# Attention feeding a mixture of experts on one core: three count operations from VectorE to GpSimd, and one router sum split over two steps

## The chip, the core and the metric

The kernel runs on one core of a Trainium2 chip. A core has five engines that run side by side and wait for each other through semaphores: PE (TensorE, matrix products into PSUM), DVE (VectorE), ACT (ScalarE), POOL (GpSimd) and SP (SyncE, which here only issues DMAs). Each engine executes its instructions in the order in which the program gives them to it. POOL also issues DMAs: those whose rows are addressed by an index (scatters and gathers), and those that add to what lies in SBUF.

The metric is the device time of one execution in microseconds; the times given are medians of several runs. The profiler records one execution more, whose span runs from its first to its last instruction.

## The reference

Eight batches of eight heads, 576 tokens each, 64 wide, go through causal attention with a decay bias. The result, 4608 rows of 512, is routed row by row to one of eight experts.

```python
def _attn_ref(q, k, v, s):
    scores = scale * np.matmul(q, k.transpose(0, 1, 3, 2))
    s_pos = np.maximum(s, 0.0)
    cum = np.cumsum(s_pos, axis=-1)
    bias = -(cum[:, :, :, None] - cum[:, :, None, :])
    scores = np.where(causal, -1000000000.0, scores + np.minimum(bias, 0.0))
    scores = scores - np.max(scores, axis=-1, keepdims=True)
    attn = np.exp(scores)
    attn = attn / (np.sum(attn, axis=-1, keepdims=True) + 1e-09)
    return np.matmul(attn, v)
...
def _moe_ref(x, expert_emb, tau, w1, w2):
    xn = x / (np.linalg.norm(x, axis=-1, keepdims=True) + 1e-06)
    en = expert_emb / (np.linalg.norm(expert_emb, axis=-1, keepdims=True) + 1e-06)
    logits = xn @ en.T / tau
    expert_idx = np.argmax(logits, axis=1)
...
    for e in range(E):
        mask = expert_idx == e
        h = np.maximum(x[mask] @ w1[e], 0.0)
        out[mask] = gate_w[mask, None] * (h @ w2[e])
```

## The kernel before

**Tiling.** A batch is called a block, `b` = 0 to 7, and a head `n` = 0 to 63, so block 7 is heads 56 to 63. The 576 query rows of a head are five tiles of 128 (the last one half full); the index `j` counts them. Four heads make a group, whose queries and keys are loaded together.

**Steps.** `step(n)` emits the work of one head for all engines, and steps follow one another. In step `n`, PE makes the transposed scores of head `n` in two PSUM tiles, `ta` and `tb` (`ta_`, `tb_`, `tbm`, `tbl`), and the scores of head `n`+5 in the other orientation, from which DVE takes the row maxima (`s1` to `s4`, `sa`, `sb`; the reductions are on lines 360, 397 and 400). ACT takes the exponentials of head `n` into one of three buffers `P32` (lines 488 and 491). POOL writes the low part of them, PL (`pl_`, line 242 by way of `psub`): 576 columns at the end of step `n`, 1024 at the beginning of step `n`+1. From step 58 on, part of the second piece is done by DVE instead (line 498). In step `n`, PE also makes the value product of head `n`-2 (`pv`, lines 516 to 518) into the PSUM bank `om`; it reads both the exponentials and PL. In step `n`+3, DVE divides the product of head `n` by its row sums (`norm1` to `norm3`, lines 529, 533, 541), writes the rows of the block (`xt`) and so frees `om` for the next product.

**DMAs of POOL.** The scores are made from high and low parts of queries and keys. The low parts come from a DMA that adds the fp32 input from DRAM to the negated rounded copy in SBUF (`addl`, line 329): for the group that comes next, into KC in the group's first step and into QC in its second one. So step 53 (second head of its group) issues the one into QC for heads 56 to 59, and step 57 the one into QC for heads 60 to 63. `ta_` and `tb_` of those heads read QC and KC on line 454.

**Router.** When the last head of block `b` has been normalised, in step 8`b`+10, `router(b, xt)` appends small tasks to a list. `slots(4)`, near the end of each step, takes up to four of them and stops at a `None`. In order: `sume` (sum of the products with the expert vectors for all five tiles, eight sums for each row; line 74, by way of `esum`), `sel1` (maximum, line 598), `None`, `sel2`, `sel3` (lines 602, 605), `None`, `sel4`, `sel5` (lines 609, 613), and `rank` into the list `mq`. `mslot`, in the middle of the next step, runs `rank`: ten small matmuls (`rank0`), and `rank1` to `rank3` go to the front of the task list, where `slots(4)` of the same step takes them. They give each row its place in its expert's table `xs` (`pos`, line 641). After that five scatters (line 659), one for each `j`, are free to be issued, one to five of them a step.

For block 5 (`b == nb - 3`) `rank1` also copies the count of expert 0 (line 633), and `rank3` works out from it the indices of the first three gathers, `cnt0`, `gi0` and `va0` (lines 643 to 645). Block 5's sum stands in step 50, its ranks in step 53. Block 6's sum stands in step 58, its ranks in step 61.

**First gathers.** In step 61, `tail` issues three gathers of expert 0's first 384 rows (`xload`, line 722), which use `gi0`; `va0` is read in `xstat`, some 30 us later. From step 56 on SP loads expert weights (line 798).

**What sets the order.** The order on each engine is the order of the program text, written out by hand (`manual_schedule`); the framework adds the waits. Near the end of step 53 the program has:

```python
        if n < NH:
            slots(4)
...
        later()
        if live and c == 0:
            addl(g + 1, True)
        if live and c == 1:
            addl(g + 1, False)
        mrow1(m)
        if live:
            pl_(n, 0, 576, "p")
```

Of the kernel before, what the change touches and what calls it, by code (L numbers as in the profile page):

```python
# [15 lines left out]
ALU = mybir.AluOpType  # L16
# [24 lines left out]
XW = 576  # L41
# [3 lines left out]
NBIG = 1 << 20  # L45
# [26 lines left out]
def esum(nc, L, x):  # L72
    e = x.rearrange("p j (q a e) -> p j e q a", q=4, e=NE)[:, :, :, :, ::17]
    nc.vector.tensor_reduce(L, e, AX.XY, ALU.add)
# [32 lines left out]
def main(ctx, tc, qkh, qkc, vtin, s_in, emb, tau, w1h, w2h, out, shared, nb):  # L107
    nc = tc.nc
# [102 lines left out]
    IX = {}  # L211
# [323 lines left out]
    def norm3(n):  # L535
        if n not in HD:
            return
        b, hh = n // H, n % H
        xt, z, ov = XT[b], HD[n]["z"], HD[n]["ov"]
        o = 72 * hh  # L540
        nc.vector.tensor_tensor(xt[:, :, o:o + 72], ov[:, :, 1 - hh % 2:73 - hh % 2], z.unsqueeze(2).to_broadcast([128, 5, 72]), op=ALU.mult)  # L541
        del HD[n]
        if hh == H - 1:
            nc.gpsimd.tensor_copy(xt[:, :, XW:XR].bitcast(I32), IX["recf"][:, b].unsqueeze(2).to_broadcast([128, 5, XR - XW]))
            nc.gpsimd.tensor_copy(xt[:, :, XW + 1:XW + 3], VB[b]["ws"].unsqueeze(1).to_broadcast([128, 5, 2]))
            router(b, xt)
# [42 lines left out]
    def router(b, xt):  # L589
        R = {}  # L590

        def sume():
            R["L"] = om[:, 416:456].rearrange("p (j e) -> p j e", j=5)
            esum(nc, R["L"], xt[:, :, 0:XW])

        def sel1():
            m = R["m"] = p2.tile([128, 2, 5], F32, name="rm", bufs=1)
            nc.vector.tensor_reduce(m[:, 0], R["L"], AX.X, ALU.max)

        def sel2():  # L600
            T = R["T"] = om[:, 456:496].rearrange("p (j e) -> p j e", j=5)
            nc.vector.tensor_tensor(T, R["L"], R["m"][:, 0].unsqueeze(2).to_broadcast([128, 5, NE]), op=ALU.is_ge)

        def sel3():
            nc.vector.tensor_tensor(R["T"], R["T"], wval, op=ALU.mult)

        def sel4():
            R["w"] = om[:, 496:501]
            nc.vector.tensor_reduce(R["w"], R["T"], AX.X, ALU.max)

        def sel5():
            oh = R["oh"] = p2.tile([128, 5, NE], BF16, name="oh", bufs=1)
            nc.vector.tensor_tensor(oh, wsel.unsqueeze(1).to_broadcast([128, 5, NE]),
                                    R["w"].unsqueeze(2).to_broadcast([128, 5, NE]), op=ALU.is_equal)

        def rank0():
            oh = R["oh"]
            pt = R["pr"] = om[:, 368:416]
            ohf = oh.rearrange("p j e -> p (j e)")
            nc.tensor.matmul(pt[:, 0:40], tri, ohf, start=True, stop=False)  # L620
            for j in range(4):
                n = 4 - j
                nc.tensor.matmul(pt[:, NE * (j + 1):40].rearrange("p (j e) -> p j e", e=NE), onesb,
                                 oh[:, j:j + 1, :].to_broadcast([128, n, NE]), start=False, stop=(j == 3))
            for j in range(5):
                nc.tensor.matmul(pt[:, 40:40 + NE], onesb, oh[:, j, :], start=(j == 0), stop=(j == 4))

        def rank1():
            nc.vector.tensor_tensor(R["T"], R["pr"][:, 0:40].rearrange("p (j e) -> p j e", j=5),
                                    base.unsqueeze(1).to_broadcast([128, 5, NE]), op=ALU.add)  # L630
            nc.vector.tensor_add(base, base, R["pr"][:, 40:40 + NE])
            if b == nb - 3:
                nc.vector.tensor_copy(IX["cnt0"][:, 0:1], base[:, 0:1])
                nc.vector.tensor_scalar(base[:, 0:1], base[:, 0:1], float(SPL), None, op0=ALU.max)

        def rank2():
            nc.vector.tensor_tensor(R["T"], R["T"], R["oh"], op=ALU.mult)

        def rank3():
            R["ps"] = p2.tile([128, 5], I32, name="pos", bufs=2)  # L640
            nc.vector.tensor_reduce(R["ps"], R["T"], AX.X, ALU.max)
            if b == nb - 3:
                nc.vector.tensor_scalar(IX["cnt0"][:, 1:2], IX["cnt0"][:, 0:1], 1.0, None, op0=ALU.subtract)
                nc.vector.tensor_scalar(IX["gi0"], IX["gp"][:, 0, 0:3], IX["cnt0"][:, 1:2], 0.0, op0=ALU.min, op1=ALU.max)
                nc.vector.tensor_scalar(IX["va0"], IX["gp"][:, 0, 0:3], IX["cnt0"][:, 0:1], float(NBIG), op0=ALU.is_ge, op1=ALU.mult)

        def rows():
            va, gp, gi = IX["va"], IX["gp"], IX["gi"]
            bb, b1 = (a.unsqueeze(2).to_broadcast([128, NE, 5]) for a in (base, IX["b1"]))
            nc.vector.tensor_max(IX["b1"], IX["b1"], base)  # L650
            vf = IX["tmp"]
            nc.vector.tensor_tensor(vf, gp, bb, op=ALU.is_ge)
            nc.vector.scalar_tensor_tensor(gi, b1, 1.0, gp, op0=ALU.subtract, op1=ALU.min)
            nc.vector.tensor_scalar(va, vf, float(NBIG), None, op0=ALU.mult)

        def scat(j):
            p = 128 if j < 4 else 64
            placed.append(b)
            ins = nc.gpsimd.indirect_dma_start(out=xs, out_offset=bass.IndirectOffsetOnAxis(ap=R["ps"][0:p, j:j + 1].bitcast(U32), axis=0),
                                         in_=xt[0:p, j].bitcast(I32), in_offset=None, bounds_check=NE * NT - 1, oob_is_err=False).ins  # L660
            for o in sent:
                tc.declare_no_dep(ins, o, reason="the ranks are distinct, so the scatters write distinct rows")
            if b > nb - 3:
                for o in firsts:
                    tc.declare_no_dep(ins, o, reason="expert 0's ranks from here on are SPL or more, the first gathers read rows below SPL")
            sent.append(ins)

        def P(f, *a):
            return lambda: f(*a)

        def rank():
            rank0()
            soon(rank1, rank2, rank3, P(late.append, P(scats.extend, sc)), *([rows] if b == nb - 1 else []))

        sc = [P(scat, j) for j in range(5)]
        tasks.extend([sume, sel1, None, sel2, sel3, None, sel4, sel5, P(mq.append, rank)])

    X, WT, HT = {}, {}, {}
    NTL = CAP // 128
# [207 lines left out]
    tasks, scats, mq, aq = deque(), deque(), deque(), deque()  # L887
# [3 lines left out]
    def soon(*fs):  # L891
        tasks.extendleft(reversed(fs))
# [573 lines left out]
```

## Time and profile before

| what | us |
|---|---|
| median of 3 runs | 770.74 (770.64 to 771.53) |
| profiled execution | 773.8 |
| its span, first to last instruction | 772.1 |
| PE busy | 757.3 |
| DVE busy | 523.7 |
| ACT busy | 567.9 |
| POOL busy | 391.4 |

The granted TensorE clock was 0.997 of full speed over the span. The attention steps run from about 20 to 350 us, the experts from there to the end; the first expert matmuls stand between the last attention steps. In the timeline each row gives the start and the duration in us, the engine, the line of the kernel, the operation, output <- input, the shapes, the number of merged instructions (x1, x2), and in brackets the idle time of the engine before it with what ended it. In the tables of waits a row gives who waited for whom, the sum in us, how often, and the longest wait.

Two things help in reading the rows. First, neighbouring instructions of DVE overlap by up to 0.1 us, so the distance between starts says more than the durations do. Second, PE's matmuls are pipelined: a row's start is what matters, and a gap is written in brackets.

### The profile page before, as it was taken

The page shows a single profiled execution, that of the slowest core. Times are in us where ns is not written, and L with a number is a line of the kernel's source. Part 1 is how long each engine was busy: PE and PEld are TensorE (multiplying, and loading weights), DVE is VectorE, ACT ScalarE, POOL GpSimd, SP SyncE. Part 2 cuts the span into 40 slices and gives each one's busy share as a digit, 9 for nine tenths or more (in the row PEclk, how much of TensorE's full clock was granted, in tenths as well). Part 3 has the DMA queues.
Part 4 walks back from the last instruction along what each step waited for, and adds up shares of the span by engine and source line. Part 5 has one row for each costly group of instructions (what it writes and reads, how often), then busy time and mean ns, then how long its engine had stood idle before and what let it go on. Part 6 is the DMA issues. An engine that isn't in the chain of part 4 may idle for free. (4 is left out here: it accounts for less than half of the span.)

```text
span 772.1 us, 19394 instructions
## 1 busy us (share of the span) xinstructions
PE 757.3 (98%) x7274; PEld 567.8 (74%) x7274; DVE 523.7 (68%) x1772; ACT 567.9 (74%) x1011; POOL 391.4 (51%) x375
## 2 busy tenths in 40 slices
PE   8899999999999999999999999999999999999997
PEld 4799999999999999985667556466475574664753
DVE  8688888888888788878577556664666466555621
ACT  9898989898989898977666767847558468375410
POOL 9997898989897989694321230221122312212001
PEclk9999999999999999999999999999999999999999
DMA  7789879797979896765444765754755558545001
GB/s 155 166 192 181 176 181 204 179 207 181 207 167 216 173 199 179 177 211 196 159 128 129 171 187 151 186 168 105 202 168 119 164 160 174 176 98 138 12 15 56
DMA packets 75980, 123.79 MB, mean 160 GB/s; under 512 B 38818, under 2 KB 39222, under 8 KB 75024
## 3 DMA queue, kind: packets, MB, share of 16 engines
q0 software_dynamic: 19632, 69.69, 38.5%
q1 hardware_dynamic: 56252, 52.84, 25.0%
q8 instruction: 58, 0.95, 0.5%
q14 instruction: 38, 0.31, 0.1%
HBM read 93.99 MB, written 21.49 MB: 150 GB/s over the span
## 5 line engine op out<-in xcount | busy, mean ns | idle before, releaser
L242 POOL TENSOR_TENSOR PL<-P 128x576 f16<-128x576 f32 (+2 forms) x128 | 204.4, 1715 | 13.5 <-ACT P L488 9.3
L854 PEld LDWEIGHTS <-wt 128*128 128x128 f16 x1536 | 149.7, 98 | 59.5 <-issue 0.5
L854 PE MATMUL h<-xH,wt 128*128 128x320 f16 (+2 forms) x1024 | 186.7, 299 | 0.0
L884 POOL DMA_INDIRECT out<-Kx,xj x39 | 41.3, 1059 | 166.6 <-DVE Kx L883 111.4
L722 POOL DMA_INDIRECT Qx<-xs,idx x40 | 42.9, 1073 | 141.1 <-ACT hp L863 84.0
L516 PE MATMUL om<-vh,P 128*128 128x73 f16 x960 | 107.4, 199 | 1.4 <-DVE xt L541 1.1
L517 PE MATMUL om<-vl,P 128*128 128x72 f16 x960 | 106.7, 197 | 0.0
L518 PE MATMUL om<-vh,PL 128*128 128x73 f16 x960 | 106.5, 198 | 0.0
L854 PE MATMUL h<-xL,wt 128*128 128x320 f16 (+1 forms) x480 | 106.1, 297 | 0.0
L352 PE MATMUL s<-qkb 96*128 96x288 f32 (+4 forms) x272 | 96.9, 370 | 2.5 <-DVE M L360 1.9
L517 PEld LDWEIGHTS <-P 128*128 128x128 bf16 x960 | 94.9, 99 | 1.6 <-issue 1.1
L878 PE MATMUL pxs<-wt,hp 128*128 128x512 f16 x351 | 94.8, 379 | 0.0
L516 PEld LDWEIGHTS <-P 128*128 128x128 bf16 x960 | 94.0, 99 | 1.1 <-DVE xt L541 0.9
L518 PEld LDWEIGHTS <-PL 128*128 128x128 f16 x960 | 94.1, 98 | 0.1
L878 PE MATMUL pxs<-wt,hq 128*128 128x512 f16 x351 | 89.0, 379 | 0.3 <-DVE wt L842 0.2
L360 DVE CUSTOM_DVE_ANT_0 junk<-s,mS 128x448 bf16<-128x448 f32 (+3 forms) x144 | 73.9, 520 | 5.7 <-PE s L352 3.5
L491 ACT ACTIVATE P<-tb 128x1024 f32<-128x1024 f32 x64 | 65.2, 1018 | 4.8 <-PE tb L457 1.9
L883 DVE TENSOR_SCALAR Kx<-pxs,xj,idx 128x512 f32<-128x512 f32 x39 | 31.5, 808 | 52.5 <-PE pxs L878 37.3
L863 ACT ACTIVATE hv<-h 128x640 f16<-128x640 f32 (+2 forms) x18 | 11.6, 644 | 73.1 <-PE h L854 63.2
L878 PEld LDWEIGHTS <-hp 128*128 128x128 f16 x351 | 34.4, 98 | 41.5 <-issue 0.5
L878 PEld LDWEIGHTS <-hq 128*128 128x128 f16 x351 | 34.4, 98 | 41.4 <-issue 0.4
L454 PE MATMUL tb<-QC,KC 128*128 128x448 f32 (+3 forms) x256 | 63.4, 307 | 0.0
(257 smaller groups left out, 1843.2 us busy)
## 6 DMA issues: line engine op xcount, KB each, us to landing
qkb<-qkh POOLq DMA_DIRECT2D x15, 1216.0 KB
ring<-w2h SPq DMA_DIRECT2D x44, 256.0 KB
ring<-w1h SPq DMA_DIRECT2D x36, 256.0 KB
KC<-qkh POOLq DMA_DIRECT2D x14, 576.0 KB
QC<-qkh POOLq DMA_DIRECT2D x14, 576.0 KB
vT<-vtin SPq DMA_DIRECT2D x24, 320.0 KB
rw<-w1h SPq DMA_DIRECT2D x15, 256.0 KB
rw<-w2h SPq DMA_DIRECT2D x12, 256.0 KB
```

What stands on the lines that cost most here:

```text
L242: nc.gpsimd.tensor_tensor(out, a, b_, op=ALU.subtract)
L352: nc.tensor.matmul(out, G[g]["QB"][0:96, h, 128 * i:128 * i + 128], G[g]["KB"][0:96, h, lo:hi], start=True, stop=True)
L360: nc.vector.tensor_tensor_reduce(out=jk, in0=src, in1=ms, scale=1.0, scalar=NEG, op0=ALU.add, op1=ALU.max, accum_out=MP[n // 2][:, n % 2, ...
L454: nc.tensor.matmul(out, HD[n]["KC"][:, ks:ks + 128], HD[n]["QC"][:, qlo:qhi], start=False, stop=stop)
L491: nc.scalar.activation(HD[n]["P32"][:, 576:1600], HD[n]["tb"], AF.Exp, scale=0.125)
L516: nc.tensor.matmul(out, lh, vh[:, kb], start=(kb == 0), stop=False)
L517: nc.tensor.matmul(out[:, u:u + 72], lh, vl[:, kb], start=False, stop=False)
L518: nc.tensor.matmul(out, ll, vh[:, kb], start=False, stop=(kb == j))
L722: ins = nc.gpsimd.indirect_dma_start(out=x.bitcast(I32), out_offset=None, in_=src, in_offset=bass.IndirectOffsetOnAxis(ap=X[("i", e, t)][1 ...
L854: nc.tensor.matmul(h[:, u, 0:b - a], w[:, 128 * c:128 * c + 128], x[:, c, lo + a:lo + b], start=(c == 0 and k == 0), stop=(c == 3 and k == 2))
L878: nc.tensor.matmul(y, h[:, 128 * t:128 * t + 128], w, start=(m == 0 and k == 0), stop=(m == 7 and k == 2))
L884: nc.gpsimd.indirect_dma_start(out=out, out_offset=bass.IndirectOffsetOnAxis(ap=xf[0].bitcast(U32), axis=0), in_=ys, in_offset=None, bound ...
```

## The change

The change has two parts.

1. In `rank3` of block 5, the three operations on the count of expert 0 (lines 643 to 645) are given to POOL instead of DVE. The copy on line 633, which they read, stays on DVE.
2. For block 6 (`b == nb - 2`) the router sum is made in two pieces, tiles 0 to 2 in step 58 and tiles 3 and 4 in step 59, with a `None` between them. `sel1` then stands in step 59, and every later task of that block one step later than before: `sel2`, `sel3` in step 60, `sel4`, `sel5` in step 61, the ranks in step 62. The scatters of that block become free at the end of step 62 instead of step 61.

```diff
-        def sume():
+        def sume(lo=0, hi=5):
             R["L"] = om[:, 416:456].rearrange("p (j e) -> p j e", j=5)
-            esum(nc, R["L"], xt[:, :, 0:XW])
+            esum(nc, R["L"][:, lo:hi], xt[:, lo:hi, 0:XW])
...
             if b == nb - 3:
-                nc.vector.tensor_scalar(IX["cnt0"][:, 1:2], IX["cnt0"][:, 0:1], 1.0, None, op0=ALU.subtract)
-                nc.vector.tensor_scalar(IX["gi0"], IX["gp"][:, 0, 0:3], IX["cnt0"][:, 1:2], 0.0, op0=ALU.min, op1=ALU.max)
-                nc.vector.tensor_scalar(IX["va0"], IX["gp"][:, 0, 0:3], IX["cnt0"][:, 0:1], float(NBIG), op0=ALU.is_ge, op1=ALU.mult)
+                nc.gpsimd.tensor_scalar(IX["cnt0"][:, 1:2], IX["cnt0"][:, 0:1], 1.0, None, op0=ALU.subtract)
+                nc.gpsimd.tensor_scalar(IX["gi0"], IX["gp"][:, 0, 0:3], IX["cnt0"][:, 1:2], 0.0, op0=ALU.min, op1=ALU.max)
+                nc.gpsimd.tensor_scalar(IX["va0"], IX["gp"][:, 0, 0:3], IX["cnt0"][:, 0:1], float(NBIG), op0=ALU.is_ge, op1=ALU.mult)
...
-        tasks.extend([sume, sel1, None, sel2, sel3, None, sel4, sel5, P(mq.append, rank)])
+        tasks.extend([*([P(sume, 0, 3), None, P(sume, 3, 5)] if b == nb - 2 else [sume]), sel1, None, sel2, sel3, None, sel4, sel5, P(mq.append, rank)])
```

## The prediction

> **What bounds the kernel now.** I read the busy row of the page first, then who TensorE (PE) waited for around the two edits, then the timeline there, engine by engine.
>
> ```profile
> PE 757.3 (98%) x7274; PEld 567.8 (74%) x7274; DVE 523.7 (68%) x1772; ACT 567.9 (74%) x1011; POOL 391.4 (51%) x375
> PE om L516 <- DVE xt L541: 1.1, 2, 0.7
> PE ta L457 <- issue: 0.3, 1, 0.3
> ```
>
> PE is busy 757.3 of 772.1 us, so nothing that leaves PE's gaps as they are can change the time. The other two rows are waits of PE between 285 and 350 us (us in total, times, longest); with the 0.41 us shown next they are 1.8 us in four gaps. Two of the four lie at the edits.
>
> The first, in step 54 (DVE, then the PE instruction that waited):
>
> ```profile
> 294.56 0.15 DVE L633 COPY idx<-base 128x1 f32<-128x1 f32 x1
> 295.05 0.20 DVE L641 TENSOR_REDUCE pos<-om 128x5 int32<-128x40 f32 x1
> 295.17 0.14 DVE L643 TENSOR_SCALAR idx<-idx 128x1 f32<-128x1 f32 x1
> 295.34 0.23 DVE L644 TENSOR_SCALAR idx<-idx 128x3 int32<-128x3 f32 x1
> 295.48 0.26 DVE L645 TENSOR_SCALAR idx<-idx 128x3 int32<-128x3 f32 x1
> 295.66 0.15 DVE L529 TENSOR_SCALAR z<-om 128x5 f32<-128x5 f32 x1
> 295.73 0.61 DVE L360 CUSTOM_DVE_ANT_0 junk<-s,mS 128x448 bf16<-128x448 f32 x1
> 296.40 0.40 PE L352 MATMUL s<-qkb 96*128 96x288 f32 x1 [0.41 <-DVE M L360]
> ```
>
> DVE works without a pause; the three count operations delay L360, which empties the score bank that the next L352 fills. PE waits 0.41 us for it.
>
> The second, in steps 58 and 59:
>
> ```profile
> 316.85 1.72 DVE L498 TENSOR_TENSOR PL<-P 128x576 f16<-128x576 f32 x1
> 320.18 0.77 DVE L74 TENSOR_REDUCE om<-xt 128x40 f32<-128x320 f32 x1
> 320.99 0.20 DVE L598 TENSOR_REDUCE rm<-om 128x5 f32<-128x40 f32 x1
> 321.10 0.15 DVE L529 TENSOR_SCALAR z<-om 128x5 f32<-128x5 f32 x1
> 321.56 0.53 DVE L541 TENSOR_TENSOR xt<-om,z 128x360 f32<-128x360 f32 x1
> 322.15 0.20 PE L516 MATMUL om<-vh,P 128*128 128x73 f16 x1 [0.42 <-DVE xt L541]
> ```
>
> DVE is the late engine again: the router sum (L74) and the maximum behind it (L598) stand ahead of the normalisation (L529 to L541) that frees the bank `om`. PE waits 0.42 us.
>
> **The change part by part.** *Counts off DVE.* L529 started at 295.66, and without the three it starts where L643 did, at 295.17: DVE is 0.49 us earlier. PE waited 0.41, so the whole gap goes, with 0.08 to spare: **-0.41 us**. The steps behind it follow PE and come 0.41 us earlier with it.
>
> *Split sum.* L74 and L598 take DVE from 320.18 to 321.10, 0.92 us. A sum of one block column is in the trace too:
>
> ```profile
> L74 DVE TENSOR_REDUCE xj<-Qx x40: 254/261/268, 358.2 to 701.2; 128x8 f32<-128x64 f32 x40
> L74 DVE TENSOR_REDUCE om<-xt x8: 742/772/781, 79.7 to 350.2; 128x40 f32<-128x320 f32 x8
> ```
>
> Five columns cost 0.772, one 0.261, so a column is (0.772 - 0.261)/4 = 0.128 and three are 0.261 + 2 x 0.128 = 0.52 us. L598 moves to step 59 with the other two columns (0.39). What stood there for 0.92 us is then 0.52, less up to 0.09 of the overlap between neighbours: DVE is 0.40 to 0.49 us earlier, against a gap of 0.42: **-0.42 us** (at worst -0.40).
>
> What is moved a step later. Step 59 gets 0.39 + 0.20 us where two operations on 128x40 stood (L602 and L605, each like L629 below): about 0.2 us more on a DVE that is by then 0.45 earlier. In step 61 the four rank operations make room for two, and in step 62 they come as an addition:
>
> ```profile
> 332.90 0.21 DVE L629 TENSOR_TENSOR om<-om,base 128x40 f32<-128x40 f32 x1 [0.38 <-PE om L518]
> 337.35 0.53 DVE L541 TENSOR_TENSOR xt<-om,z 128x360 f32<-128x360 f32 x1
> 339.53 0.20 PE L516 MATMUL om<-vh,P 128*128 128x73 f16 x1
> ```
>
> Four like L629 are at most 4 x 0.21 = 0.84 us of DVE. Added ahead of L541 of step 63, they move its end from 337.88 to 338.72, and PE needs it at 339.53: 0.81 us of cover, cost nothing (without that cover 0.84). The ten small rank matmuls move with it, the same number. The five scatters of block 6 start one step later (none in step 62, two in 63, three in 64): the next reader of those rows is a gather behind block 7's scatters, at 360 us. Nothing.
>
> *The counts on GpSimd* are the dear part. POOL executes in order, and the step's queue is: rest of PL, **the three counts**, the accumulating DMA into QC, PL of the step, then the scatters. The counts need L633, which ends at 294.71. POOL before:
>
> ```profile
> 290.70 1.39 POOL L329 DMA_DIRECT2D QC<-qkh  x1
> 291.36 3.75 POOL L242 TENSOR_TENSOR PL<-P 128x576 f16<-128x576 f32 x2
> 295.54 1.11 POOL L659 DMA_INDIRECT xs<-xt,pos  x1 [0.44 <-DVE idx L643]
> 308.33 3.44 POOL L242 TENSOR_TENSOR PL<-P 128x576 f16<-128x576 f32 x2
> 311.27 1.52 POOL L329 DMA_DIRECT2D QC<-qkh  x1
> 316.80 1.15 POOL L242 TENSOR_TENSOR PL<-P 128x576 f16<-128x576 f32 x1 [1.56 <-ACT P L488]
> L544 POOL COPY xt<-idx 128x20 int32<-128x20 int32 x8 | 5.2, 652 | 0.0
> L237 POOL TENSOR_SCALAR wsel<-base 128x8 f32<-128x8 f32 x1 | 0.2, 192 | 0.1
> ```
>
> The DMA issued at 290.70 and the PL pair of 291.36 now stand behind a wait that ends at 294.71. The trace shows no such count on POOL. Nearest are a tensor-scalar at 0.19 (L237) and a small integer copy at 0.65 (L544): three are 0.57 to 1.95 us. I take 0.25 each, near L237, which is the same operation, and 0.1 for gaps: 0.85. The DMA then goes out at 294.71 + 0.85 = 295.56 instead of 290.70, the PL pair ends at 295.56 + 0.66 + 3.75 = 299.97, and the scatters begin there instead of 295.54: **POOL is 4.4 us late**. Its first wait for another engine after 295.54 is the 1.56 us ahead of 316.80, so it stays 4.4 us late until the waits from step 58 on let it catch up.
>
> [...]
>
> Is there cover for 4.4 us? PL is needed by the value product two steps on:
>
> ```profile
> 317.60 0.21 PE L516 MATMUL om<-vh,P 128*128 128x73 f16 x1
> 324.16 0.43 PE L454 MATMUL ta<-QC,KC 128*128 128x320 f32 x2
> ```
>
> The tightest: PL of head 56 ended at 308.33 + 3.44 = 311.77 and now ends at 316.2; PE needs it at 317.60 - 0.41 = 317.19. 1.0 us is left. The heads before it have more. With 0.65 us per count POOL is 5.5 us late, and this cover is gone to within 0.1 us.
>
> The second DMA that is late is the one at 311.27, into QC for heads 60 to 63: now at 315.7, read by L454 at 324.16 - 0.83 = 323.33, so it has 7.6 us. How long one takes, from the DMA share and bytes:
>
> ```profile
> vh<-w1h SPq DMA_DIRECT2D x2, 256.0 KB
> 314.97 1.38 SPq L798 DMA_DIRECT2D vh<-w1h  x2
> 319.56 0.33 SPq L798 DMA_DIRECT2D mS<-w1h  x1
> 294.00:296.00 2.00, 1.99 (x16) 1.77 (x12) 1.83 (x12) 1.98 (x5) 1.56 (x2) 1.00 1.07 197
> 296.00:298.00 2.00, 1.60 (x15) 1.60 (x16) 1.75 (x7) 1.65 (x2) 1.68 (x2) 1.00 0.75 208
> 318.00:320.00 2.00, 2.00 (x45) 1.97 (x42) 1.83 (x8) 2.00 (x3) 0.93 (x1) 1.00 1.04 352
> 322.00:324.00 2.00, 1.85 (x48) 1.84 (x48) 2.00 (x4) 1.97 (x5) 2.00 (x2) 1.00 0.02 5
> ```
>
> In the window rows the last two columns are the DMA share and GB/s. The one of 290.70 kept the engines full to about 296 to 297, 5.3 to 6.3 us from issue. So the late one lands at 321 to 322, but now beside five transfers of expert weights (the first and the last are shown; the 352 GB/s row), which before came after it. I take it as just in time. For group 14 there are 9 us of room.
>
> **Sum** against the profiled execution: 772.1 - 0.41 - 0.42 = 771.27 us of span (773.8 with what lies around it, to 773.0). The runs shown have a median of 770.74, below that execution, so the same 0.83 us gives 769.91.
>
> **The rivals.**
> *A, one gap comes back.* DVE gets only 0.08 us more than the first gap and about nothing more than the second; a hand-over that I mis-sized leaves one of them. For: the thin margins. Against: both instructions before the gap are plain DVE chains. 772.1 - 0.42, so 770.3.
>
> *B, POOL's queue becomes the bound (slower).* Place: the accumulating DMA for heads 60 to 63. The five weight transfers, 1.28 MB, at 352 GB/s hold the DMA engines for 3.6 us; if the DMA waits for all of them it lands at 322 + 3.6 = 325.6, 2.3 us too late, one for one on PE: -0.83 + 2.3 = +1.5, so 772.2. With 0.65 us per count it is 1.1 us worse, 773.3. It is slower than before from the point where the landing takes more than 8.4 us from issue. Against: the engines share among queues, and were idle by 322 (0.02).
>
> *C, POOL blocks DVE.* L498 takes 1.72 us at 316.85 behind a POOL L242 that began at 316.80, and it is followed by everything up to the second gap; here is one that found POOL free:
>
> ```profile
> 325.37 0.75 DVE L498 TENSOR_TENSOR PL<-P 128x576 f16<-128x576 f32 x1
> ```
>
> So L498 seems to wait for the running L242 (316.80 + 1.15 = 317.95, then 0.62). POOL, late, now works through this stretch without a pause; were L498 to wait for two such (1.15 + 0.93), DVE would lose 1.0 us, and the second gap would be 0.42 + 1.0 - 0.45 = 0.97: -0.41 + 0.55 = +0.14, so 770.9. Against: at 316.85 it already has nearly the whole wait for one. [...]
>
> *D, more than these two gaps.* If the freed DVE also closed the gaps of 0.3 and 0.7: 772.1 - 1.8, so 768.9. Against: neither follows the moved work.
>
> **How the numbers follow.** Forecast 0.60 (769.91, itself 769.5 to 770.3), A 0.15, B 0.13, C 0.07, D 0.05. A measurement of this kernel can tell about 0.2% from no change, 1.54 us: below 769.2 or above 772.28. Only D, with a little from noise, is faster by that: 0.06. B's upper half is slower by that: 0.07. The rest, 0.87, is no change. Range: 769.0 (D almost) to 772.0 (B up to near its centre); beyond it lie about 2 in 10.
>
> **What would show it.** Right: L360 of step 54 about 0.5 us earlier against PE, both gaps (0.41 before L352, 0.42 before L516) gone; three POOL tensor-scalars at about 294.8 with some 3.6 us of POOL idle ahead of them; L329 at 295.6 and 315.7; POOL caught up by 322. Wrong: a PE wait on POOL's PL at steps 57 or 58, or on a DMA into QC at step 60 (B); L498 of step 58 above 2 us (C); POOL idle-free at 291 to 295, which would mean the counts do not stand where I read them.

## The result, and the profile after

| | us | ratio to before |
|---|---|---|
| before | 771.13 (770.61 to 772.1, 6 runs) | |
| after | 775.55 (774.22 to 776.26, 6 runs) | 1.0052 (1.0042 to 1.0062) |

The change makes the kernel 4.4 us slower, where 0.8 us faster was forecast. The profiled execution of after took 776.26 us, 774.5 of them its span.

The busy row of the page of after, and the waits of PE between 285 and 352 us:

```profile
PE 758.1 (98%) x7274; PEld 568.6 (73%) x7274; DVE 526.7 (68%) x1770; ACT 568.2 (73%) x1011; POOL 390.7 (50%) x378
```

```profile
PE ta L454 <- DMA QC<-qkh: 2.0, 1, 2.0
PE tb L450 <- DVE M L360: 1.1, 1, 1.1
PE om L516 <- DVE xt L541: 0.4, 1, 0.4
PE V L290 <- DVE vl L301: 0.4, 1, 0.4
```

PE is busy for 0.8 us more, so the loss is time in which it waits. Both gaps that the change aimed at are gone; none of these four is one of them. The two large ones in the timeline of PE, with the first matmul of steps 59, 60 and 61 (L457):

```profile
318.57 0.27 PE L457 MATMUL ta<-trim,identb 128*128 128x256 bf16 x1
320.43 0.62 PE L450 MATMUL tb<-qkb 128*128 128x448 f32 x2 [1.05 <-DVE M L360]
324.12 0.28 PE L457 MATMUL ta<-trim,identb 128*128 128x256 bf16 x1
326.69 0.50 PE L454 MATMUL ta<-QC,KC 128*128 128x320 f32 x2 [2.04 <-DMA QC<-qkh]
330.52 0.27 PE L457 MATMUL ta<-trim,identb 128*128 128x256 bf16 x1
```

The distance between two such L457 is PE's time for a step (step 59: 324.12 - 318.57 = 5.55). Beside them stand those of a second profile of before (771.58 us, span 769.8), and of three experiments told below. The last column runs from the L457 of step 63 to the start of the last ACT instruction (L1431).

| us for step | 54 | 55 to 58 | 59 | 60 | 61 | 62 | 63 to the end |
|---|---|---|---|---|---|---|---|
| before | 5.78 | 19.44 | 4.65 | 4.12 | 4.23 | 4.12 | 430.03 |
| after | 5.30 | 19.43 | 5.55 | 6.40 | 3.91 | 4.44 | 431.15 |
| counts alone | 5.29 | 19.43 | 5.90 | 6.07 | 4.24 | 4.11 | 430.00 |
| split alone | 5.78 | 19.44 | 4.30 | 4.11 | 3.91 | 4.44 | 431.17 |
| counts in step 58, and split | 5.29 | 19.42 | 4.28 | 4.12 | 3.90 | 4.44 | 431.13 |

After gains 0.5 us in step 54, loses 0.9 + 2.3 us in steps 59 and 60, and 1.1 us behind step 62: 3.8 us in all. The 0.32 us that leave step 61 for step 62 are the ten moved rank matmuls. The medians differ by 4.4 us, and the 0.6 us between that and the 3.8 was not traced. (The two profiles differ by another 1.0 us ahead of step 54, which starts at 293.84 in after and at 292.87 in the second profile of before. The programs are the same up to step 53, and the granted clock between 36 and 38 us was 0.50 in after and 0.97 in the other, so this part is hardly the change's.) How the loss in steps 59 and 60 comes about is to be seen on POOL:

```profile
294.74 0.25 POOL L643 TENSOR_SCALAR idx<-idx 128x1 f32<-128x1 f32 x1 [3.71 <-DVE idx L633]
295.09 0.27 POOL L644 TENSOR_SCALAR idx<-idx 128x3 int32<-128x3 f32 x1
295.43 0.35 POOL L645 TENSOR_SCALAR idx<-idx 128x3 int32<-128x3 f32 x1
295.83 1.10 POOL L329 DMA_DIRECT2D QC<-qkh  x1
296.56 3.40 POOL L242 TENSOR_TENSOR PL<-P 128x576 f16<-128x576 f32 x2
...
312.95 3.48 POOL L242 TENSOR_TENSOR PL<-P 128x576 f16<-128x576 f32 x2
315.89 1.53 POOL L329 DMA_DIRECT2D QC<-qkh  x1
316.60 3.42 POOL L242 TENSOR_TENSOR PL<-P 128x576 f16<-128x576 f32 x2
```

POOL sits idle for 3.71 us at the head of the three counts, and everything behind them is late: the DMA into QC for heads 60 to 63 goes out at 315.89 instead of 311.27, and releases PE at 326.69, 10.8 us later. And POOL has two L242 in a row at 316.60, where it had one and then an idle stretch. DVE beside it:

```profile
316.29 2.97 DVE L498 TENSOR_TENSOR PL<-P 128x576 f16<-128x576 f32 x1
...
320.87 0.53 DVE L74 TENSOR_REDUCE om<-xt 128x24 f32<-128x192 f32 x1
...
336.01 4.67 DVE L498 TENSOR_TENSOR PL<-P 128x576 f16<-128x576 f32 x1
...
341.19 0.19 DVE L629 TENSOR_TENSOR om<-om,base 128x40 f32<-128x40 f32 x1
```

L498 of step 58 takes 2.97 us (1.72 before), and L400 and L360, which free the bank for the next L450, stand behind it: PE's 1.05 us. L498 of step 62 takes 4.67 us (1.01 in the second profile of before), ahead of L301 and the rank operations: the two waits of 0.4 us.

### The profile page after: what moved, and what is told of

Same layout as the page of the kernel before. It is cut to its first block, busy times and chain, and to the rows that moved or that the text cites. A ratio compares the mean times of both kernels' runs of the same rounds, so it can differ in the third digit from the quotient of the medians.

```text
span 774.5 us, 19397 instructions
## 1 busy us (share of the span) xinstructions
PE 758.1 (98%) x7274; PEld 568.6 (73%) x7274; DVE 526.7 (68%) x1770; ACT 568.2 (73%) x1011; POOL 390.7 (50%) x378
## 5 line engine op out<-in xcount | busy, mean ns | idle before, releaser
L242 POOL TENSOR_TENSOR PL<-P 128x576 f16<-128x576 f32 (+2 forms) x128 | 204.2, 1715 | 10.7 <-ACT P L488 7.1
L516 PE MATMUL om<-vh,P 128*128 128x73 f16 x960 | 108.1, 200 | 1.0 <-DVE xt L541 0.4
L516 PEld LDWEIGHTS <-P 128*128 128x128 bf16 x960 | 94.4, 99 | 0.7 <-DVE xt L541 0.4
L360 DVE CUSTOM_DVE_ANT_0 junk<-s,mS 128x448 bf16<-128x448 f32 (+3 forms) x144 | 73.9, 520 | 5.4 <-PE s L352 3.2
L454 PE MATMUL tb<-QC,KC 128*128 128x448 f32 (+3 forms) x256 | 63.4, 307 | 0.0
```

The source lines that it names most:

```text
L242: nc.gpsimd.tensor_tensor(out, a, b_, op=ALU.subtract)
L360: nc.vector.tensor_tensor_reduce(out=jk, in0=src, in1=ms, scale=1.0, scalar=NEG, op0=ALU.add, op1=ALU.max, accum_out=MP[n // 2][:, n % 2, ...
L454: nc.tensor.matmul(out, HD[n]["KC"][:, ks:ks + 128], HD[n]["QC"][:, qlo:qhi], start=False, stop=stop)
L516: nc.tensor.matmul(out, lh, vh[:, kb], start=(kb == 0), stop=False)
```

## The experiments

The theory after this reading (**queue**): the price is POOL's wait for L633, through what stands behind it. Rivals: the loss comes from the split sum; from the three operations themselves; or from DVE and POOL blocking each other (**port**; the name stands for that alone, and no run shows by what means they would block each other). Runs are told in groups of one chip; each ratio is to runs of before on the same chip.

**Which part, and is it the wait?** One part alone, and then two kernels on the wait.

Counts alone (the first part of the change):

> The change without the split sum: the three counts on POOL in step 53, the router sum of block 6 whole. Queue theory (the counts' wait for L633 holds back everything behind them on POOL, so a DMA into QC and a PL piece come late): as slow as the whole change or 0.4 us more, ratio to before 1.004 to 1.006; the trace keeps a PE wait on the DMA into QC of about 2 us in step 60 and the L498 of step 58 of about 3 us. Operation theory (small elementwise work costs more on POOL, or blocks DVE): the same 1.005. Moved-chain theory (the cost is the split sum and the rank chain one step later): 0.9995, the first gap of 0.41 us gone and nothing added.

Split alone (the second part):

> The change without its first part: the counts stay on DVE, only the sum of block 6 is split. Queue theory and operation theory: ratio 0.9995 (-0.42 us, the gap before L516 in step 59 gone, the gap of 0.41 before L352 in step 54 still there), no PE wait on a DMA. Moved-chain theory: 1.004 to 1.006.

Counts on POOL where nothing waits for L633, at the end of step 58, with the split:

```diff
-            if b == nb - 3:
-                nc.gpsimd.tensor_scalar(IX["cnt0"][:, 1:2], ...
...
+        if n == NH - 6:
+                nc.gpsimd.tensor_scalar(IX["cnt0"][:, 1:2], ...
```

> The whole change, but the three counts stand on POOL at the end of step 58, behind PL, where L633 is long done and POOL has idle time; they are still POOL instructions. Queue theory: both gaps go and nothing is late, ratio 0.999 (-0.8 us), no PE wait on the DMA into QC, L498 of step 58 at 1.7 us or less. Operation theory: still 1.004 to 1.006. Moved-chain theory: 1.004 to 1.006.

The kernel before, with one small copy on POOL that reads L633's output at that place in step 53; nothing reads what it writes:

```diff
                 nc.vector.tensor_scalar(IX["va0"], ...
+                nc.gpsimd.tensor_copy(IX["spare"], IX["cnt0"][:, 0:1])
```

> The kernel before, with one extra tiny copy on POOL at the place of the counts in step 53, which reads what L633 writes and is read by nothing; the counts stay on DVE, the sum is whole. Queue theory: the wait alone does it, POOL idle 3.7 us ahead of the copy, the DMA into QC and PL some 4 us late, ratio 1.003 to 1.006 with both small gaps still there. Operation theory: one copy of 0.2 us, 1.000. Moved-chain theory: 1.000.

| | us | ratio |
|---|---|---|
| counts alone | 775.36 | 1.0057 (1.0034 to 1.0079) |
| split alone | 772.25 | 1.0011 (1.0002 to 1.0019) |
| counts in step 58, and split | 771.37 | 0.9999 (0.9990 to 1.0007) |
| one waiting copy | 777.25 | 1.0075 (1.0061 to 1.0089) |

PE's waits, of the counts alone and then of the counts in step 58:

```profile
PE ta L454 <- DMA QC<-qkh: 1.7, 1, 1.7
PE tb L450 <- DVE M L360: 1.1, 1, 1.1
PE om L516 <- DVE xt L541: 0.6, 2, 0.4
```

```profile
PE om L516 <- DVE xt L541: 0.5, 1, 0.5
PE V L290 <- DVE vl L301: 0.4, 1, 0.4
```

The counts alone bring both large waits and, in the table of steps, all that is lost in steps 59 and 60 and nothing behind it. The same three operations on the same engine, five steps later, bring none of it: it is their place, not their duration. Three of the four forecasts were met only in part. The split alone was to gain (0.9995) and loses 0.1%, and the counts in step 58 with the split stay short of 0.999; the two waits left in the second list are what both lose, and they are taken up below. The waiting copy lost more than the 1.006 forecast. POOL and then DVE with the one waiting copy (lines are shifted by one or two):

```profile
292.94 0.19 POOL L647 COPY idx<-idx 128x1 f32<-128x1 f32 x1 [3.67 <-DVE idx L634]
...
294.09 3.37 POOL L243 TENSOR_TENSOR PL<-P 128x576 f16<-128x576 f32 x2
```

```profile
293.51 3.98 DVE L645 TENSOR_SCALAR idx<-idx 128x3 int32<-128x3 f32 x1
```

A single copy of 0.19 us costs 5.8 us. It does so partly in another way than the change: the pair of L243 that it delays now meets the count still on DVE, which takes 3.98 us instead of 0.23 and holds PE for 4.1 us (s L353). Step 54 takes 12.36 us in this run against 5.78 before; the part of it beyond the wait goes with the granted clock, which was 0.50 from 298 to 304 us, where the second profile of before has 1.00. PE, by then late itself, does not wait for QC. In the changed kernel that count is no longer on DVE. So this run shows that the wait alone is enough to lose several us, not that it loses them on the same road.

**The two waits behind the queue.** All three start from after: the DMA into QC moved from the end of step 57 to its beginning; no L498 in step 58 (POOL makes that piece of PL); both.

```diff
             ta_(n, m)
+        if n == NH - 7:
+            addl(g + 1, False)
...
-        if live and c == 1:
+        if live and c == 1 and n != NH - 7:
```

```diff
     def PS(n):
-        return 1024 if NH - 7 < n < NH - 1 else 1600
+        return 1024 if NH - 6 < n < NH - 1 else 1600
```

> The whole change, with one line moved: the DMA into QC for heads 60 to 63 is issued at the start of step 57, ahead of PL's second piece, instead of at its end. Theory that the landing of this DMA is what PE waits for in step 60: it goes out about 3 us earlier, the wait of 2.0 us is gone, the 1.05 us gap behind the 2.97 us L498 of step 58 stays, ratio to before 1.002 to 1.003. Rival (what holds PE is DVE behind L498, and the DMA is late only beside the weights in any case): 1.005, as the change.

> The whole change, with the DVE part of PL in step 58 (L498) given back to POOL. If L498 waits for POOL's running PL pieces, the DVE gap of 1.05 us goes; but PE then stands 1 us earlier before the DMA into QC, which lands when it did, so that wait grows from 2.0 to about 3.1 us: ratio 1.005, unchanged. If the two waits add, 1.0038.

> Both edits together: the early DMA into QC and no L498 in step 58. Both waits go (2.0 and 1.05 us), what is left against before is the second half of the change, in which the scatters moved out of step 62 leave POOL's PL pieces back to back and the L498 of step 62 took 4.67 us: ratio 1.000 to 1.0015. If something else of the change holds PE, 1.003 or more.

| | us | ratio | L450 waits for L360 | L454 waits for QC |
|---|---|---|---|---|
| QC early | 773.31 | 1.0027 (1.0017 to 1.0037) | 0.81 | none |
| no L498 in step 58 | 774.89 | 1.0049 (1.0035 to 1.0063) | none | 2.90 |
| both | 773.31 | 1.0029 (1.0018 to 1.0039) | none | 1.58 |

Issue and release of QC, on POOL and PE, first without that L498 and then with both edits:

```profile
314.92 1.53 POOL L329 DMA_DIRECT2D QC<-qkh  x1
```

```profile
325.26 0.50 PE L454 MATMUL ta<-QC,KC 128*128 128x320 f32 x2 [2.90 <-DMA QC<-qkh]
```

```profile
312.36 1.55 POOL L329 DMA_DIRECT2D QC<-qkh  x1
```

```profile
323.25 0.50 PE L454 MATMUL ta<-QC,KC 128*128 128x320 f32 x2 [1.58 <-DMA QC<-qkh]
```

The two waits stand one behind the other for the same time. Where DVE no longer holds PE, PE comes to the DMA earlier and waits the difference there (1.05 + 2.04 = 3.1 us in after, 2.9 without L498). So the third run missed its forecast: without L498, even the early issue comes too late, and nothing is won over moving the DMA alone. In both of these the DMA takes 10.3 and 10.9 us from issue to release, as against 10.8 in after. An earlier issue halves the loss; it does not take away what else is late in POOL's queue.

**What the split gives back.** In the table of steps the split alone gains 0.35 us in step 59 (the gap aimed at) and loses 1.1 behind step 62. PE's waits with the split alone:

```profile
PE om L516 <- DVE xt L541: 0.5, 1, 0.5
PE V L290 <- DVE vl L301: 0.4, 1, 0.4
PE s L352 <- DVE M L360: 0.4, 1, 0.4
```

The last is the gap of step 54, still there. The first two are new and stand behind an L498 of step 62 that takes 4.69 us. Two causes are possible: that this L498 is held by POOL (port), since the scatter that stood between POOL's pairs in step 62 has moved away; or that the moved rank operations are late wherever L498 stands (load). The yardstick is a second profile of before, taken beside the last three runs. Then come, on another chip, three kernels with the counts in step 58: split with the rank chain left in step 61; no split; and split with the chain moved, without the L498 of step 62.

> The kernel before, unchanged, for a second profiled execution: the first one took 773.8 us where the runs' median is 771. If the two gaps of 0.41 and 0.42 us belong to the program, both stand here again; what the first profile had beyond them (a gap of 0.4 at 260 to 280 us, 0.66 at 342.85) may not. Expected span 769 to 770 us.

This came out as expected: a span of 769.8 us, the two gaps again (0.40 and 0.43 us), and one of 0.21 us beyond them.

```diff
-        tasks.extend([*([P(sume, 0, 3), None, P(sume, 3, 5)] if b == nb - 2 else [sume]), sel1, None, ...
+        tasks.extend([P(sume, 0, 3), None, P(sume, 3, 5), sel1, sel2, sel3, sel4, sel5, P(mq.append, rank)] if b == nb - 2 else ...
```

> Counts on POOL at the end of step 58, and the sum of block 6 split, but without moving the chain behind it: step 59 takes the second piece, the maximum and both selections, so that the ranks stand in step 61 and the first scatter in step 62 as before. Port theory (the scatters moved out of step 62 leave POOL's PL pieces back to back, the L498 of that step is held for 4.6 us and costs about 1 us on PE in steps 62 and 63): L498 of step 62 at about 1 us, both first gaps gone, ratio 0.9987 to 0.999. If the split itself costs (more DVE instructions, another place in the order): 1.000, as with the counts late and the chain moved.

> Only the counts, on POOL at the end of step 58; the sum whole, the chain where it was. Step 54 loses its gap of 0.41 us, step 59 keeps its own: ratio 0.9994. If the gap comes back elsewhere, 1.000.

```diff
-        return 1024 if NH - 7 < n < NH - 1 else 1600
+        return 1024 if NH - 7 < n < NH - 2 else 1600
```

> Counts late, sum split and chain moved as in the change, but the DVE part of PL in step 62 given to POOL, so that there is no L498 to be held in that step. Port theory: the waits of 0.4 us on L301 and L541 in steps 62 and 63 go, about 1 us is won against the run with the counts late, ratio 0.9985 to 0.999. If the moved rank chain itself is what costs (four more DVE operations ahead of L541 of step 63), the loss stays: 0.9995 to 1.0005.

| (before here: 773.76 us) | us | ratio | L498 of step 62 |
|---|---|---|---|
| split, chain in place | 775.74 | 1.0026 (1.0015 to 1.0037) | 4.26 |
| no split | 773.56 | 0.9993 (0.9984 to 1.0001) | 0.75 |
| split, chain moved, without L498 | 773.82 | 1.0001 (0.9992 to 1.0010) | none |

The first missed both its forecasts, the second met its own, and the third came out where load had it (0.9995 to 1.0005) and not where port had it. With the chain in place, the scatter is back between POOL's pairs, and L498 is held all the same. POOL and DVE there:

```profile
333.89 1.03 POOL L655 DMA_INDIRECT xs<-xt,pos  x1 [0.18 <-DVE z L533]
334.95 3.00 POOL L242 TENSOR_TENSOR PL<-P 128x576 f16<-128x576 f32 x2
```

```profile
334.32 4.26 DVE L498 TENSOR_TENSOR PL<-P 128x576 f16<-128x576 f32 x1
```

It began at 334.32, and its 0.75 us would have ended at 335.07, after POOL's pair had begun. Without the split it ran from 334.43 to 335.18, and the pair began at 335.27. So the end that L498 would have had lies 0.12 us behind the start of the pair in one run and 0.09 us ahead of it in the other, and the durations are 3.5 us apart; that this distance decides was not shown. The 2.0 us that this run loses were traced only in part, by PE's waits:

```profile
PE om L517 <- issue: 0.9, 2, 0.5
PE V L290 <- DVE vl L301: 0.6, 1, 0.6
```

The wait for L301 stands behind the held L498. The first row is two gaps in step 61 for which the profile names no releaser; the run without the split, on the same chip, has one of 0.5 us there. In the third run the waits on L301 and L541 of the table above are gone, but the moved chain waits itself:

```profile
332.62 0.18 PE L620 MATMUL om<-oh,tri 128*128 128x40 bf16 x1 [0.41 <-DVE xt L541]
```

Its step 62 takes 5.00 us, against 4.44 with the held L498. So it speaks for load: with no L498 to be held, the moved chain still costs what the split gains. A last group, on a third chip: the yardstick again, split with the chain in place and without that L498, and the kernel before without that L498 as its control.

> The kernel with the counts on GpSimd at the end of step 58, the sum split, and the rank chain one step later, once more, as the yardstick of the two beside it. Both theories: 0.9995 to 1.0005, with L498 of step 62 at 4.6 us and waits of about 0.4 us for L301 and L541.

> Counts on GpSimd at the end of step 58, sum split, ranks in step 61 and scatters in step 62 as before the change, and no L498 in step 62 (GpSimd makes that part of PL; the sums are the same). Theory 'port': what the split sum gains is lost in step 62 because L498 is held by GpSimd's back-to-back operations; without L498 there both gains stay, -0.8 us, 0.9987 to 0.9992, and no wait of PE for L301 or L541 in steps 61 to 63. Theory 'load': GpSimd or VectorE has too much to do in steps 61 to 63 wherever it stands; then a wait of 0.4 us or more stands there again, 0.9997 or above.

> The kernel before with no L498 in step 62, the control for the run beside it. Both theories: L498 of step 62 took 0.75 us there and held nothing up, so 0.9995 to 1.0005; if it is faster by 0.05% or more, a gain of the run beside it is partly due to this and not to the split.

| | us | ratio | steps 54 to 62 | step 63 to the end |
|---|---|---|---|---|
| counts in step 58, split, chain moved | 771.79 | 1.0004 (0.9995 to 1.0013) | 41.47 | 431.52 |
| the same, chain in place, no L498 in 62 | 771.73 | 0.9997 (0.9988 to 1.0006) | 41.47 | 430.99 |
| before, no L498 in 62 | 772.20 | 1.0007 (0.9998 to 1.0016) | 42.35 | 430.66 |

The second run missed port's forecast of 0.9987 to 0.9992 and stands at load's bound of 0.9997; the control missed its 1.0005. (Its forecast gives L498 of step 62 as 0.75 us in the kernel before; it is 0.80 and 1.01 in the two profiles, and 0.75 in the run without the split.) Against the control it is 0.9997/1.0007 = 0.9990, though the two intervals overlap, and the stages say how: 0.88 us won up to step 63 (both gaps), 0.33 lost behind it. One of PE's waits in the second run has about the size of that loss, and the control does not have it:

```profile
PE pxs L744 <- DVE wt L752: 0.4, 1, 0.4
```

The first wins the same 0.88 and loses 0.86. So both theories hold a part. The held L498 together with the moved chain is where most of the split's gain goes, and how much falls to each of the two was not separated. The other 0.33 us goes with DVE being late at L752, with neither a held L498 nor a moved chain, as load has it. Leaving L498 out is no way to keep the gain, since POOL then has 576 columns more to make and the control itself came out slower, if within its interval.

No version beat the kernel before by more than can be measured. The best is the counts at the end of step 58 without the split, 0.9993.

## Why the prediction was wrong, point by point

- **Counts off DVE, -0.41: right.** Step 54 is 0.48 us shorter in after, and in every run with the counts off DVE: the whole gap, and a little more.
- **Split sum, -0.42: right in its place.** The sum of three columns took 0.53 us (0.52 worked out), the gap before L516 of step 59 is gone, and step 59 is 0.35 us shorter with the split alone, where 0.42 was forecast.
- **POOL 4.4 us late: right.** The counts took 0.25 + 0.27 + 0.35 = 0.87 us (294.74 to the DMA at 295.83, so 1.1 with gaps, against 0.85), the DMA went out at 295.83 (295.56), the one for heads 60 to 63 at 315.89 (315.7), the first scatter at 300.15 instead of 295.54, so 4.6 us late. On DVE the three had taken 0.14 + 0.23 + 0.26 = 0.63, so the ratio is 1.4. PE waited for no PL, as the 1.0 us of cover said.
- **The step that failed: the landing of the DMA into QC.** "So the late one lands at 321 to 322 ... I take it as just in time." It was given 5.3 to 6.3 us from issue, read off the DMA share around a transfer that had run before the weight loads began. It took 10.7 us to land, and PE waited 2.04 us for it. The page of the second profile of before has landing times (count, size, median us from issue to landing):

```profile
QC<-qkh POOLq DMA_DIRECT2D x14, 576.0 KB, 7.8
```

  The two transfers that the prediction looked at took 7.8 us each there, issued at 289.64 and 310.23. So the term was 1.5 us or more too small for the old place already, and 2.9 us more came with the new one. The prediction had seen the five weight transfers and set the point at 8.4 us; it then chose the shorter time, because "the engines share among queues, and were idle by 322". They were idle by 322 because the DMA had gone out 3.7 us ahead of the first of those five (311.27 against 314.97) and had landed. In after it goes out 1.5 us behind the first of them (315.89 against 314.41) and meets the rest:

```profile
316.00:318.00 2.00, 2.00 (x41) 2.00 (x38) 2.00 (x2) 1.95 (x3) 2.00 (x4) 1.00 1.10 225
318.00:320.00 2.00, 1.37 (x27) 1.14 (x23) 1.83 (x4) 2.00 (x4) 2.00 (x3) 1.00 1.09 336
320.00:322.00 2.00, 1.57 (x12) 1.54 (x13) 1.85 (x9) 1.08 (x3) 1.94 (x5) 1.00 0.92 160
322.00:324.00 2.00, 1.93 (x47) 1.73 (x46) 1.70 (x4) 1.97 (x4) 2.00 (x2) 1.00 1.11 245
324.00:326.00 2.00, 0.66 (x12) 0.42 (x8) 1.69 (x7) 1.50 (x5) 1.00 (x2) 1.00 0.80 198
```

  The DMA share is 0.8 or more to the end, where the stretch from 322 showed 0.02 before. By queue, SP's packets had 104 and 96% of the engines' time in the us from 318 and from 319, POOL's 0.3 and 17%; in those from 322 and 323 POOL's had 78 and 83%, SP's 27 and 28%. So the two queues do share the engines, but for 2 us the weights had nearly all of them. That the weights are what lengthened the transfer is read from these rows and shares; no run moved them. Rival B had this wait, at 2.3 us.
- **Rival C's bound failed as well.** "At 316.85 it already has nearly the whole wait for one" took one POOL operation as the most that L498 waits for. It waited through two pieces, those that begin at 316.60 and 317.71: L498 ended at 319.26, and POOL's next operation had started at 318.59. It took 2.97 us, and PE lost 1.05. (The row of the pair ends only at 320.02, so rows of POOL overlap here by 1.43 us.) B and C were priced as alternatives; they have one cause and came together.
- **"Nothing" for the moved chain and scatters failed.** The cover of 0.81 us ahead of L541 of step 63 was reckoned from the four rank operations alone. In step 62, which has no scatter any more, POOL's four L242 ran on end, L498 was held for 4.67 us ahead of them, and PE waited 0.42 us for L301 and 0.45 for L541. With the split alone the 1.1 us behind step 62 are more than the gap was worth.

The forecast of -0.83 is what the edits do to DVE's list of work. What they do to POOL's order stands against it: 3.6 us in steps 59 and 60 through the counts' place (5.55 + 6.40 against 4.28 + 4.12 with the counts in step 58), and 1.1 us behind step 62 through the split. Rival A's lost gap and D's two more gaps did not come about.

## What to carry to other kernels

Before an operation is given to another in-order engine, look at what stands behind it there while it waits for its input, DMAs above all: the wait of three operations of 0.3 us cost 3.7 us of the whole queue, and putting them where their input had long been ready cost nothing. Price a delayed DMA by what the DMA engines do at its new time, not by how long it took at its old one (10.7 us here against 7.8), and take its length from a landing on record, not from the share of busy DMA engines (which gave 5.3 to 6.3). An engine that is made to catch up may work without gaps, and those gaps may be what another engine lives on: from 311.28 to 325.00 POOL waited for no other engine in after, where it had waits of 1.56, 1.08 and 1.77 us before, and DVE's L498 took 2.97 us there instead of 1.72.

## What the runs showed of the hardware

**DVE can be held through a whole run of POOL operations, but is not always.** POOL with the counts in step 58 (last group), and DVE beside it:

```profile
329.81 4.99 POOL L242 TENSOR_TENSOR PL<-P 128x576 f16<-128x576 f32 x4
```

```profile
330.78 4.64 DVE L498 TENSOR_TENSOR PL<-P 128x576 f16<-128x576 f32 x1
```

POOL's run ends at 329.81 + 4.99 = 334.80, L498 at 335.42, 0.62 us behind it; in after it is 335.08 + 4.98 = 340.06 and 340.68, again 0.62. With POOL free it takes 0.75. So here it is held through four operations of POOL that follow each other. The 128x3 tensor-scalar with the waiting copy was held through two: it ended at 297.49, POOL's pair at 297.46. In step 59 of the second profile of before it went otherwise:

```profile
320.68 2.55 POOL L242 TENSOR_TENSOR PL<-P 128x576 f16<-128x576 f32 x2 [1.77 <-ACT P L488]
```

```profile
320.98 1.47 DVE L498 TENSOR_TENSOR PL<-P 128x576 f16<-128x576 f32 x1
```

POOL's second piece starts at 321.79, and L498 ends at 322.45, 0.78 us before the pair does. It got in behind the first piece, and POOL waited: the pair took 2.55 us, a pair of the same size with no L498 beside it 2.05 (first profile of before, at 332.33).

The order of the starts alone does not tell which engine gets in first: two DVE operations that began ahead of POOL's pair lost to it (L498 at 334.32 against 334.95 with the split and the chain in place, and the 128x3 operation at 293.51 against 294.09 with the waiting copy). POOL was issuing a DMA when these two began, but an L498 at 334.43 in the run without the split ran beside a scatter in its 0.75 us. What decides is open.

**The same DMA of 576 KB landed after 5.8 us in one place and after 11.5 in another.** It took 5.8 and 6.2 us where the DMA engines had been nearly idle (with the waiting copy, issued at 293.43; in after, at 295.83; DMA share 0.06 and 0.04 there), 7.8 at the old place of the one for heads 60 to 63, and 10.2 to 10.8 beside the weights. One issued at 272.7 in after, ahead of the weight loads (the first of these at 304.57), took 11.5, with a DMA share of 0.77 to 1.11 in the windows from 272 to 284 us, so weights are not the only thing that makes it long.

**PE's clock was halved behind a wait of 4.1 us.** With the one waiting copy PE waited 4.1 us up to 298.28, and its granted clock was 0.50 in the windows from 298 to 304 us; its value matmuls started 0.06 us apart there, 0.03 before the wait. Behind the wait of 2.90 us (no L498 in step 58, up to 325.26) it was 1.00 throughout, from 322 to 330 us.
